# An attention kernel with a computed position bias: relus taken off GpSimd, the pair step's order of issue changed, the opening and the first weight conversions rearranged

## The chip, the cores and the metric

The kernel runs on one core of a Trainium2 chip. The metric is the device time of one execution in microseconds (us). The engines are named as the profile names them: PE (TensorE, matrix products and transposes), DVE (VectorE), ACT (ScalarE), POOL (GpSimd), and SP, whose queue issues nearly all DMAs.

## The reference, cut to what matters

```python
# attention: B, H, S, D = 2, 8, 576, 64
scores = (q @ k^T) / sqrt(D)
psi_rel = log1p(abs(pos[:, None] - pos[None, :]))
psi_i = log1p(maximum(pos[:, None], 1.0))
h = maximum((psi_rel / psi_i)[..., None] @ w1 + b1, 0.0)   # 32 hidden values for each pair of positions
scores = scores + (h @ w2)                                 # 8 heads, one bias for both batches
attn = exp(scores - max); attn = attn / (sum(attn) + 1e-09)
x = attn @ v                                               # 1152 tokens x 512
# two feed-forward layers after it
x = ((x @ w_a) * (x @ w_b)) @ w_out                        # d_ff 1536
hh = x @ w_in; solu = hh * softmax(hh)                     # d_ff 1024
out = layernorm(solu) * g_ln @ w_out2
```

The feed-forward weights come in 64-bit words and are converted on the chip. Products that must be exact in 32 bits are taken as three products of split values, a high part and the rest.

## The kernel before, in words

The bias is made tile by tile, 36 tiles T = 0 to 35 of 16 positions each. For a tile, `bias_hidden(T)` writes four arrays `h` of 128 x 576: a shifted window of a table `tabs` plus one scalar per partition, then a relu. The table `HIDDEN` says which engine makes each of the four: "v" is DVE, "p" POOL (both L365), "a" ACT (L363). `bias_sums(T)` multiplies them with w2 on PE into a PSUM tile `bps` (16 matmuls, L373). `bias_out(T)` evicts it with ACT into `st` (L383), and a DMA on the SP queue writes it into the bias array of its 128 rows (L385). Eight tiles make one such array.

The opening loop makes T = 0 to 8 and, between them, seven pieces of transposed q and k: `piece` transposes on PE into the one PSUM tile of the pool `ps_t` (tag t), `high` rounds it on ACT to the high part (`qhi`, `khi`, L308), and `lower` subtracts on DVE for the rest (`qlo` L317, `klo` L313). Then the SP queue gets the DMAs for the next q, the k of batch 1 and the v.

The main loop has 39 steps m, one for a pair of heads of one unit (128 rows of one batch; the ninth unit holds the last 64 rows of both batches). Software pipelining spreads a pair over four steps: in step m the scores, bias and exponentials of pair m, the reciprocal and shares of pair m - 1, the transposes of pair m - 2, and the values product of pair m - 3. Each engine works in the order in which the code issues. In a step with a bias tile, this order is:

- PE: scores of the first head (L401), scores of the second head, tail transposes (L439) and transposes of the next q (L275) into the second head's tile, sixteen transposes into `pt` (L450), values into `px` (L482), bias sums (L373).
- DVE: `biased` for both heads (scores plus bias with a running minimum, L415), the reciprocal of pair m - 1 (L428), half of `et` (L464), `qlo` (L317), the relus of the next tile (L365).
- ACT: exponential of the first head (L422), `ett` (L455), `qhi` (L308), exponential of the second head, half of `et` (L464), a relu of the next tile (L363), the eviction `st` (L383).
- POOL: the add before the reciprocal (L427), the two shares `e` times `rec` (L433), a relu (L365).

The pool `ps_s` has two PSUM tiles (tag s), and each step takes three in turn: the first head's scores, the second head's, and the bias sums. The second head's scores take the tile that the bias sums of the step before held, so they wait for its eviction.

```python
for T in range(N0 + 1):          # opening, N0 = 8
    bias_hidden(T)
    if T > 0:
        bias_sums(T - 1)
        bias_out(T - 1)
```

When a unit's fourth values product is done, `inputs_high` rounds `px` with ACT (`xhi`, L488) and `inputs_low` subtracts with DVE (`xlo`, L493), both at the end of the same step. `EARLY` puts three blocks of the first feed-forward product (`gated`, matmuls of L128) into the last steps; for them four pieces of w_a and w_b are converted in the late steps by `first_one`, in six stages each, placed by `FIRST` in half steps (64 is step 32): load, `held` on ACT (L94), `brought` (clamp, L98) with a first bit operation (L107), two more bit operations on DVE (L109, L110), the high part on ACT (L577), the rest on DVE (L579). After the loop the feed-forward part runs with PE as its steady user.

Of the kernel before, what the change touches and what calls it, by code (L numbers as in the profile page):

```python
# [17 lines left out]
P = 128  # L18
# [10 lines left out]
HIDDEN = (("pvav", "vvav", "pvva", "pvvv"),)  # L29

LOADS = ((0, 1), (1, 1), (2, 2), (3, 2))
FIRST = ((-7, -5, -3, 1, 2, 3), (-6, -4, -2, 3, 4, 5), (-5, 0, 2, 5, 6, 7), (2, 4, 5, 6, 8, 9))
# [18 lines left out]
def tile_kernel(ctx, tc, q, k, v, w1, b1, w2, w_a, w_b, w_out, w_in2, w_out2, g_ln, psi, rpsi, out):  # L51
# [108 lines left out]
    with ExitStack() as actx:  # L160
# [158 lines left out]
        def piece(w):  # L319

            src, at, g, c = w
            ps = ps_t.tile([P, 2, 512], F32, tag="t", name=f"tp_{'_'.join(map(str, w))}")
            nat = fetched[w]
            if src == "q":
                turn(ps, 0, nat, range(HG))
                return q_views(at, g, 0, ps, 0) + q_views(at, g, 1, ps, 2 * HF), -scale
            turn(ps, 0, nat, range(HG), (0, 1) if c < NK else (at,))
            return k_views(at, g, c, ps, 0), 1.0
# [19 lines left out]
        def bias_hidden(T, engines="vpa"):  # L348

            it, r, c = place(T)  # L350
            kinds = HIDDEN[min(it, len(HIDDEN) - 1)]
            kinds = kinds[T % len(kinds)]
            hs = bias_w.setdefault(T, [None] * 4)
            for qd in range(4):
                e = kinds[qd]
                if e not in engines:
                    continue
                t0 = it * P + r + 16 * qd
                h = hp.tile([P, S], F32, tag="h", name=f"h_{T}_{qd}")
                win = tb[:, OFF - t0 - c:OFF - t0 - c + S]  # L360
                sc = nb[:, c, t0 // 16:t0 // 16 + 1]
                if e == "a":
                    nc.scalar.activation(h, win, AF.Relu, bias=sc)  # L363
                else:
                    (nc.vector if e == "v" else nc.gpsimd).tensor_scalar(h, win, sc, 0.0, op0=ALU.add, op1=ALU.max)  # L365
                hs[qd] = h
# [147 lines left out]
        for T in range(N0 + 1):  # L514
            if T == N0 - 2:
                halves_l = table(low, half - low, psi_l, low - 12, ps_s, "s")
                nc.scalar.copy(*halves_l[0])
                nc.vector.tensor_copy(*halves_l[1])
            bias_hidden(T)
            if T > 0:  # L520
                bias_sums(T - 1)
                bias_out(T - 1)
            if done:
                lower(*done)
                done = None
            if T > 0 and order:
                done = piece(order.pop(0))
                high(*done)
# [3 lines left out]
        if done:  # L532
            lower(*done)
        bias_sums(N0)
        bias_out(N0)
        for g in range(2):
            fetch(("q", 1, g, 0))
        for w in ks[1][:3]:
            fetch(w)
        for p in range(-1, 2):  # L540
            load_v(0, p)
        for w in ks[1][3:]:
            fetch(w)
        for p in range(2, HP):
            load_v(0, p)

# [16 lines left out]
        def first_one(i):  # L563
# [6 lines left out]
            held(words, f)  # L570
            yield
            brought(f, nc.vector)
# [6 lines left out]
            nc.vector.tensor_tensor(out=lo, in0=f, in1=hi.bitcast(F32), op=ALU.subtract)  # L579
# [22 lines left out]

        bias_hidden(sums_at[0])
        NP = len(pairs)
        for m in range(NP + LAG + 1):
# [21 lines left out]
            if now:  # L627
                biased(u, 2 * p)
                powers(u, 2 * p)
                biased(u, 2 * p + 1)  # L630
            if last:
                summed_powers(*last)
            if up:
# [7 lines left out]
            if up:  # L641
                turned(*up)
            if out_:
                values(*out_)
            if T is not None:
                bias_sums(T)
            if up:
                kept(*up, 1)
                kept(*up, 0)
            lower(views, -scale)  # L650
# [3 lines left out]
            if T is not None:  # L654
                bias_out(T)
# [4 lines left out]
            if out_ and out_[1] == HP - 1:  # L660
                inputs_high(out_[0])
                inputs_low(out_[0])
            if now and p > 1 and u + 2 < NU:
                fetch(("q", u + 2, p - 2, 0))
            others(2 * m + 1)

# [340 lines left out]
```

## Time and profile before

| | |
|---|---|
| median of three runs | 570.29 us (570.04 to 570.39) |
| the profiled execution | 570.18 us, span 568.2 us |
| mean granted TensorE clock | 0.976 |
| busy, share of the span | PE 90%, DVE 74%, ACT 50%, POOL 36% |

The span runs from the first to the last instruction; 2.0 us of the execution lie around it. Busy shares are means over an opening, an attention loop and a feed-forward part with different limits, so the stretches are read one by one.

### The profile page before, as it was taken

To read this page: it belongs to the slowest core of one execution; us is meant where nothing else is said; L and a number is where in the kernel's file an instruction comes from. 1 tells how busy PE (TensorE), PEld (TensorE's weight loads), DVE (VectorE), ACT (ScalarE), POOL (GpSimd) and SP (SyncE) were. 2 spreads that over 40 slices of the span, in tenths; PEclk is the share of its full clock that TensorE was granted. 3 is DMA by queue.
4 is the path that set the end of the run, shared out by engine and by line. 5 is a ranking of instruction groups with operands and counts; after the bars stand their busy time and mean duration, and the time that the engine had idled before them with its cause. 6 is when DMAs were issued, how large, how long until landed. Compare 5 with 4: busy or idle time off the path is not lost.

```text
span 568.2 us, 13476 instructions
## 1 busy us (share of the span) xinstructions
PE 513.5 (90%) x5416; PEld 448.9 (79%) x5416; DVE 420.6 (74%) x864; ACT 281.4 (50%) x607; POOL 201.8 (36%) x235
## 2 busy tenths in 40 slices
PE   5766888888877986999999999999999999999997
PEld 2334666666665876999999999999999988888886
DVE  4847888978986596369789889889785566765661
ACT  4745787777776654345555524451352533223231
POOL 5815667666656444022222212224121630000000
PEclk9987999989999798999999999999999999999999
DMA  5469543333355410064444434345320000000001
GB/s 130 123 154 220 116 102 84 85 80 84 84 117 136 127 40 2 2 197 146 142 148 149 148 112 149 112 144 153 112 76 1 0 1 18 20 19 20 20 18 55
DMA packets 63521, 51.75 MB, mean 91 GB/s; under 512 B 41182, under 2 KB 53731, under 8 KB 63460
## 3 DMA queue, kind: packets, MB, share of 16 engines
q1 hardware_dynamic: 63184, 50.88, 32.7%
q8 instruction: 42, 0.69, 0.5%
q14 instruction: 19, 0.16, 0.1%
q10 hardware_dynamic: 276, 0.02, 0.0%
HBM read 36.73 MB, written 2.36 MB: 69 GB/s over the span
## 4 chain that ended last, share of the span: by engine, by line
PE 67%; DVE 14%; ACT 10%; issue 4%; DMA 2%; SPq 1%; POOL 1%; DVEq 0%; ACTq 0%; POOLq 0%
PE pm L128 25%; PE po L128 13%; PE py L904 9%; PE ph L844 9%; DVE e L415 4%; DVE h L365 4%; ACT st L383 3%; PE s L401 2%; PE bps L373 2%; PE px L482 2%; ACT h L363 2%; DVE qlo L317 2%; ACT et L464 2%; ACT e L422 1%; PE pl L885 1%
## 5 line engine op out<-in xcount | busy, mean ns | idle before, releaser
L98 POOL TENSOR_SCALAR f<-f 128x512 f32<-128x512 f32 x48 | 41.3, 861 | 142.7 <-ACT f L94 135.9
L433 POOL TENSOR_SCALAR e<-e,rec 128x576 f32<-128x576 f32 x72 | 55.1, 778 | 70.6 <-DVE rec L428 70.6
L128 PE MATMUL pm<-xhi,abh 128*128 128x384 f32 x240 | 80.2, 334 | 0.0
L128 PE MATMUL pm<-xhi,abl 128*128 128x384 f32 x240 | 80.2, 334 | 0.0
L128 PE MATMUL pm<-xlo,abh 128*128 128x384 f32 x240 | 80.2, 334 | 0.0
L422 ACT ACTIVATE e<-e,nm 128x576 f32<-128x576 f32 x72 | 55.9, 776 | 43.0 <-DVE nm L415 31.4
L365 POOL TENSOR_SCALAR h<-tabs 128x576 f32<-128x576 f32 x27 | 64.9, 2406 | 8.2 <-PE bps L373 5.4
L415 DVE CUSTOM_DVE_ANT_0 e<-s,bias 128x576 f32<-128x576 f32 x72 | 52.6, 751 | 20.6 <-PE s L275 14.0
L365 DVE TENSOR_SCALAR h<-tabs 128x576 f32<-128x576 f32 x90 | 62.7, 745 | 2.8 <-PE bps L373 2.8
L373 PE MATMUL bps<-h,w2bd 128*32 128x288 f32 x576 | 47.2, 446 | 3.2 <-POOL h L365 3.1
L128 PE MATMUL po<-gh,oh 128*128 128x384 f32 x144 | 48.5, 337 | 0.6 <-DVE x2s L775 0.6
L128 PE MATMUL po<-gh,ol 128*128 128x384 f32 x144 | 48.4, 336 | 0.0
L128 PE MATMUL po<-gl,oh 128*128 128x384 f32 x144 | 48.4, 336 | 0.0
L128 PEld LDWEIGHTS pm<-xhi,abh 128*128 128x128 f32 x240 | 45.1, 188 | 0.0
L128 PEld LDWEIGHTS pm<-xlo,abh 128*128 128x128 f32 x240 | 45.1, 188 | 0.0
L128 PEld LDWEIGHTS pm<-xhi,abl 128*128 128x128 f32 x240 | 45.1, 188 | 0.0
L401 PE MATMUL s<-khi,qhi 64*128 64x288 f32 x128 | 26.0, 400 | 20.8 <-ACT st L383 17.9
L401 PEld LDWEIGHTS s<-khi,qhi 64*128 64x128 f32 x128 | 12.6, 190 | 40.6 <-ACT st L383 24.6
L110 DVE SCALAR_TENSOR_TENSOR f<-words,f 128x512 int32<-128x512 int32 x48 | 42.9, 893 | 1.6
L147 ACT COPY one<-pm 128x384 f32<-128x384 f32 x36 | 17.1, 476 | 50.3 <-PE pm L128 50.3
L482 PE MATMUL px<-et,vsb 128*32 128x128 f32 (+1 forms) x1280 | 41.5, 275 | 0.0
L94 ACT ACTIVATE f<-words 128x512 f32<-128x512 f32 x48 | 32.4, 676 | 17.9 <-DMA words<-in_moe_w_out_dram 6.9
(149 smaller groups left out, 1247.6 us busy)
## 6 DMA issues: line engine op xcount, KB each, us to landing
bias<-st SPq DMA_DIRECT2D x40, 288.0 KB, 3.5
words<-in_moe_w_out_dram SPq DMA_DIRECT2D x20, 512.0 KB, 3.6
words<-in_moe_w_a_dram SPq DMA_DIRECT2D x12, 512.0 KB, 3.6
words<-in_moe_w_b_dram SPq DMA_DIRECT2D x12, 512.0 KB, 3.6
nat_q<-in_q_dram SPq DMA_DIRECT2D x32, 128.0 KB, 3.5
words<-in_moe_w_in_dram SPq DMA_DIRECT2D x8, 512.0 KB, 3.6
arena<-in_k_dram SPq DMA_DIRECT2D x16, 128.0 KB, 3.9
vsb<-in_v_dram SPq DMA_DIRECT2D x16, 128.0 KB, 3.0
```

The lines of the kernel that those rows point to most:

```text
L98: engine.tensor_scalar(f, f, WORD_MAX, WORD_MIN, op0=ALU.min, op1=ALU.max)
L110: nc.vector.scalar_tensor_tensor(out=b, in0=words[:, :, 0], scalar=29, in1=b, op0=ALU.logical_shift_right, op1=ALU.bitwise_or)
L128: nc.tensor.matmul(ps, w, x, start=(i == 0), stop=(i == n - 1))
L365: (nc.vector if e == "v" else nc.gpsimd).tensor_scalar(h, win, sc, 0.0, op0=ALU.add, op1=ALU.max)
L373: nc.tensor.matmul(bps[32 * qd:32 * qd + 32, a, 0:SH], w2bd, h[:, a * SH:(a + 1) * SH], start=True, stop=True)
L401: nc.tensor.matmul(ps[:, a, 0:SH], w[r], x[r, b, h, :], start=(i == 0), stop=(i == len(mm) - 1))
L415: nc.vector.tensor_tensor_reduce(out=halves(e), in0=ps[:, :, 0:SH], in1=halves(bias_t[it][:, h, :]), op0=ALU.add, op1=ALU.min, scale=1.0, ...
L422: nc.scalar.activation(e, e, AF.Exp, bias=nm, scale=-1.0, accum_out=sums[:, h:h + 1])
L433: nc.gpsimd.tensor_scalar(e, e, rec[:, h:h + 1], 1.0, op0=ALU.mult, op1=ALU.mult)
L482: nc.tensor.matmul(px[rows, p, cols], lhsT, rhs, start=(c == 0 and m == 0), stop=(c == NC), skip_group_check=True)
L844: nc.tensor.matmul(ph[u][:, a], x[:, kc, cols], w[:, kc, a * 512:(a + 1) * 512], start=(i == 0), stop=(i == 3 * KD - 1))
L904: nc.tensor.matmul(ps, x[:, c, :], w[:, c, cols], start=(i == 0), stop=(i == 3 * KF - 1))
```

## The change

Five edits. No relu is made on POOL any more: `HIDDEN` holds only "v" and "a", with a row of its own for the first eight tiles. In the pair step the bias sums go ahead of the values on PE, the eviction of the sums goes ahead of half of `et` and the relu on ACT, and `inputs_low` moves into the next step. The reciprocal goes between the two `biased` of DVE. The opening loop ends at T = 7 and makes only four of the seven pieces in it; the other three, tile 8 and the DMAs are issued after it. In `first_one`, the clamp and the last subtraction go to GpSimd, and the stages are placed anew.

```diff
--- before.py
+++ after.py
@@ -26,10 +26,10 @@
 
 LAG = 2
 
-HIDDEN = (("pvav", "vvav", "pvva", "pvvv"),)
+HIDDEN = (("vvva", "vava", "vvva", "vavv", "vvva", "vavv", "vvva", "vavv"), ("vvav", "vvvv", "vavv", "vvva"))
 
 LOADS = ((0, 1), (1, 1), (2, 2), (3, 2))
-FIRST = ((-7, -5, -3, 1, 2, 3), (-6, -4, -2, 3, 4, 5), (-5, 0, 2, 5, 6, 7), (2, 4, 5, 6, 8, 9))
+FIRST = ((-7, -5, -4, -1, 0, 1), (-6, -4, -2, 1, 2, 3), (-5, -2, 0, 3, 4, 5), (0, 2, 4, 6, 7, 8))
 
 
 SUMS = (6, 5, 5)
@@ -316,10 +316,10 @@
                 for l_, p_, h_ in parts_:
                     nc.vector.scalar_tensor_tensor(out=l_, in0=p_, scalar=by, in1=h_.bitcast(F32), op0=ALU.mult, op1=ALU.subtract)
 
-        def piece(w):
+        def piece(w, pool=ps_t, tag="t"):
 
             src, at, g, c = w
-            ps = ps_t.tile([P, 2, 512], F32, tag="t", name=f"tp_{'_'.join(map(str, w))}")
+            ps = pool.tile([P, 2, 512], F32, tag=tag, name=f"tp_{'_'.join(map(str, w))}")
             nat = fetched[w]
             if src == "q":
                 turn(ps, 0, nat, range(HG))
@@ -345,24 +345,21 @@
             it, r = divmod(T, P // 16)
             return it, 64 * (r // 4), r % 4
 
-        def bias_hidden(T, engines="vpa"):
+        def bias_hidden(T):
 
             it, r, c = place(T)
             kinds = HIDDEN[min(it, len(HIDDEN) - 1)]
             kinds = kinds[T % len(kinds)]
             hs = bias_w.setdefault(T, [None] * 4)
             for qd in range(4):
-                e = kinds[qd]
-                if e not in engines:
-                    continue
                 t0 = it * P + r + 16 * qd
                 h = hp.tile([P, S], F32, tag="h", name=f"h_{T}_{qd}")
                 win = tb[:, OFF - t0 - c:OFF - t0 - c + S]
                 sc = nb[:, c, t0 // 16:t0 // 16 + 1]
-                if e == "a":
+                if kinds[qd] == "a":
                     nc.scalar.activation(h, win, AF.Relu, bias=sc)
                 else:
-                    (nc.vector if e == "v" else nc.gpsimd).tensor_scalar(h, win, sc, 0.0, op0=ALU.add, op1=ALU.max)
+                    nc.vector.tensor_scalar(h, win, sc, 0.0, op0=ALU.add, op1=ALU.max)
                 hs[qd] = h
 
         def bias_sums(T):
@@ -511,38 +508,50 @@
             fetch(w)
         N0 = P // 16
         done = None
-        for T in range(N0 + 1):
-            if T == N0 - 2:
-                halves_l = table(low, half - low, psi_l, low - 12, ps_s, "s")
-                nc.scalar.copy(*halves_l[0])
-                nc.vector.tensor_copy(*halves_l[1])
+        for T in range(N0):
             bias_hidden(T)
             if T > 0:
                 bias_sums(T - 1)
                 bias_out(T - 1)
+            if T == N0 - 2:
+                halves_l = table(low, half - low, psi_l, low - 12, ps_t, "t")
+            if T == N0 - 1:
+                nc.scalar.copy(*halves_l[0])
+                nc.vector.tensor_copy(*halves_l[1])
             if done:
                 lower(*done)
                 done = None
-            if T > 0 and order:
+            if T > 0 and len(order) > 3:
                 done = piece(order.pop(0))
                 high(*done)
             if T == 1:
                 for j in range(2):
                     nc.gpsimd.memset(vtl[(1 - j) * TL:(2 - j) * TL, :, :, j, :], 0.0)
-        if done:
-            lower(*done)
-        bias_sums(N0)
-        bias_out(N0)
+        assert done is None and len(order) == 3
+        bias_sums(N0 - 1)
+        bias_out(N0 - 1)
+        for w in ks[1][:2]:
+            fetch(w)
         for g in range(2):
             fetch(("q", 1, g, 0))
-        for w in ks[1][:3]:
-            fetch(w)
         for p in range(-1, 2):
             load_v(0, p)
-        for w in ks[1][3:]:
+        for w in ks[1][2:]:
             fetch(w)
         for p in range(2, HP):
             load_v(0, p)
+        bias_hidden(N0)
+        made = piece(order[0])
+        high(*made)
+        lower(*made)
+        made = piece(order[1])
+        high(*made)
+        lower(*made)
+        bias_sums(N0)
+        made = piece(order[2])
+        high(*made)
+        lower(*made)
+        bias_out(N0)
 
         sums_at, keys_at, extra = {}, {}, {}
 
@@ -568,15 +577,15 @@
             yield
             f = pools[0].tile([P, NW], F32, tag="gl" if i < 3 else "gh", name=f"single_{i}")
             held(words, f)
+            brought(f, nc.gpsimd)
             yield
-            brought(f, nc.vector)
             yield from single(words, f)
             if not first:
                 first.append(big.tile([P, 2, 2, 2, NW], F32R, tag="big", name="first"))
             hi, lo = (first[0][:, j, c, m] for j in range(2))
             nc.scalar.copy(hi, f)
             yield
-            nc.vector.tensor_tensor(out=lo, in0=f, in1=hi.bitcast(F32), op=ALU.subtract)
+            nc.gpsimd.tensor_tensor(out=lo, in0=f, in1=hi.bitcast(F32), op=ALU.subtract)
             if m == 1:
                 w_ab[c] = tuple([first[0][:, j, c, l].rearrange("p (k f) -> p k f", k=KD) for l in range(2)] for j in range(2))
             yield
@@ -600,6 +609,7 @@
             for f, args in extra.pop(n, []):
                 f(*args)
 
+        gone = []
         bias_hidden(sums_at[0])
         NP = len(pairs)
         for m in range(NP + LAG + 1):
@@ -627,9 +637,10 @@
             if now:
                 biased(u, 2 * p)
                 powers(u, 2 * p)
-                biased(u, 2 * p + 1)
             if last:
                 summed_powers(*last)
+            if now:
+                biased(u, 2 * p + 1)
             if up:
                 kept_tails(*up, spare)
             high(views, -scale)
@@ -640,29 +651,33 @@
                     shares(last[0], 2 * last[1] + h)
             if up:
                 turned(*up)
+            if T is not None:
+                bias_sums(T)
             if out_:
                 values(*out_)
-            if T is not None:
-                bias_sums(T)
             if up:
                 kept(*up, 1)
+            lower(views, -scale)
+            if gone:
+                inputs_low(gone.pop())
+            if T is not None:
+                bias_out(T)
+            if up:
                 kept(*up, 0)
-            lower(views, -scale)
             others(2 * m)
             if after is not None:
                 bias_hidden(after)
-            if T is not None:
-                bias_out(T)
             for w in keys_at.get(m, []):
                 made = piece(w)
                 high(*made)
                 lower(*made)
             if out_ and out_[1] == HP - 1:
                 inputs_high(out_[0])
-                inputs_low(out_[0])
+                gone.append(out_[0])
             if now and p > 1 and u + 2 < NU:
                 fetch(("q", u + 2, p - 2, 0))
             others(2 * m + 1)
+        inputs_low(gone.pop())
 
 
     w2p = ctx.enter_context(tc.tile_pool(name="w2p", bufs=1, side="right"))
```

## Rows read from the trace of the kernel before

**Rows 1.** Stages: length; busy (count) of PE, PEld, DVE, ACT, POOL; clock; DMA
```profile
0.00:33.71 33.71, 22.21 (x280) 10.61 (x280) 20.15 (x41) 18.38 (x31) 22.30 (x22) 0.95 0.53 127
33.71:60.94 27.23, 18.51 (x246) 12.85 (x246) 18.45 (x45) 16.17 (x36) 10.29 (x12) 0.81 0.82 179
60.94:178.29 117.35, 98.42 (x2084) 76.96 (x2085) 102.05 (x246) 88.45 (x206) 80.21 (x88) 0.99 0.42 97
178.29:189.03 10.74, 7.70 (x134) 6.32 (x131) 5.24 (x17) 5.24 (x15) 3.84 (x8) 0.75 0.67 178
189.03:212.77 23.74, 20.67 (x462) 18.07 (x460) 19.75 (x49) 15.30 (x41) 11.42 (x20) 0.97 0.20 59
212.77:220.82 8.05, 4.22 (x122) 3.52 (x122) 5.36 (x14) 3.83 (x9) 1.66 (x3) 1.00 0.01 2
```
**Rows 2.** Groups by line, 60.94 to 178.29: count, busy, mean ns, idle before
```profile
L365 DVE TENSOR_SCALAR h<-tabs 128x576 f32<-128x576 f32 x55 | 41.0, 793 | 0.0
L365 POOL TENSOR_SCALAR h<-tabs 128x576 f32<-128x576 f32 x17 | 40.9, 2405 | 0.0
...
L401 PE MATMUL s<-khi,qhi 64*128 64x288 f32 x92 | 18.4, 396 | 18.8 <-ACT st L383 17.3 <-DVE qlo L317 1.5
```
**Rows 3.** Timeline of two steps: start, length, engine, what, idle before and releaser
```profile
105.88 0.74 DVE L415 CUSTOM_DVE_ANT_0 e<-s,bias 128x576 f32<-128x576 f32 x1
...
106.25 0.40 PE L401 MATMUL s<-khi,qhi 64*128 64x288 f32 x2 [0.71 <-ACT st L383]
...
107.14 0.76 DVE L415 CUSTOM_DVE_ANT_0 e<-s,bias 128x576 f32<-128x576 f32 x1 [0.51 <-PE s L275]
...
108.08 1.46 POOL L433 TENSOR_SCALAR e<-e,rec 128x576 f32<-128x576 f32 x2 [0.69 <-DVE rec L428]
...
108.65 1.19 PE L373 MATMUL bps<-h,w2bd 128*32 128x288 f32 x16
...
108.99 2.21 DVE L365 TENSOR_SCALAR h<-tabs 128x576 f32<-128x576 f32 x3
...
109.52 2.41 POOL L365 TENSOR_SCALAR h<-tabs 128x576 f32<-128x576 f32 x1
...
111.12 0.74 DVE L415 CUSTOM_DVE_ANT_0 e<-s,bias 128x576 f32<-128x576 f32 x1
...
112.01 0.19 POOL L427 TENSOR_SCALAR rec<-sums 128x2 f32<-128x2 f32 x1
...
113.71 1.70 DVE L365 TENSOR_SCALAR h<-tabs 128x576 f32<-128x576 f32 x2
...
116.32 0.69 DVE L493 TENSOR_TENSOR xlo<-px,xhi 128x512 fp32r<-128x512 f32 x1 [0.90 <-ACT xhi L488]
```
**Rows 4.** Timeline of the opening up to the first pair step
```profile
9.24 2.17 PE L373 MATMUL bps<-h,w2bd 128*32 128x288 f32 x16 [3.15 <-POOL h L365]
...
18.87 1.20 PE L373 MATMUL bps<-h,w2bd 128*32 128x288 f32 x16
...
22.48 0.94 DVE L365 TENSOR_SCALAR h<-tabs 128x576 f32<-128x576 f32 x2
...
29.53 0.74 ACT L383 ACTIVATE st<-bps,rp 128x576 f32<-128x576 f32 x1 [1.00 <-ACT h L363]
...
32.23 2.47 SPq L256 DMA_DIRECT2D nat_q<-in_q_dram  x4
...
36.82 0.48 PE L275 MATMUL s<-ident,nat_q 64*128 64x64 f32 x4 [4.49 <-DMA nat_q<-in_q_dram]
```
**Rows 5.** Timeline around the last pair step
```profile
217.49 0.69 DVE L493 TENSOR_TENSOR xlo<-px,xhi 128x512 fp32r<-128x512 f32 x1 [2.62 <-ACT xhi L488]
...
221.63 0.69 PE L128 MATMUL pm<-xhi,first 128*128 128x384 f32 x1 [3.57 <-DVE nm L415]
```
**Rows 6.** Groups by line, whole span: the conversions' subtraction on DVE, a like one on POOL
```profile
L924 POOL TENSOR_TENSOR wo_lo<-wo,wo_hi 128x512 fp32r<-128x512 f32 x8 | 10.4, 1297 | 9.3 <-ACT wo_hi L923 9.3
...
L579 DVE TENSOR_TENSOR first<-single,first 128x512 fp32r<-128x512 f32 x4 | 2.7, 685 | 0.1
```

## The prediction

> **What bounds the kernel now.** I read the table of stages first, cut where the first biased operation of steps 0, 4, 27, 29, 34 and 35 starts [rows 1]. What lies behind 220.82 is feed-forward work that the change does not touch, so it moves as a block. Ahead of it no engine is full. From step 4 to step 27, 23 steps take 117.35 us, 5.10 each, of which PE is busy 4.28 (98.42 / 23), DVE 4.44, ACT 3.85 and POOL 3.49. So the loop is tied by waits between engines with nearly equal loads, DVE nearest to full.
>
> The groups by line say which waits [rows 2]. PE's first matmul of a score waits 17.3 us in that stretch for the eviction `st`. DVE's relus have a mean of 793 ns, POOL's 2405. The timeline of two steps shows how this closes a loop [rows 3]: ACT evicts the sums late, the second head's scores start at 106.25 after 0.71 of waiting, and DVE stands 0.51 at 107.14 for these scores. Then DVE makes its relus beside POOL's shares and relu: three in 2.21, or two in 1.70. Once per unit it also waits 0.90 for `xhi` before `xlo` (116.32). In the opening, the timeline shows PE waiting 3.15 for POOL's first relu, and 4.49 for the next q, whose DMAs stand behind the bias DMAs [rows 4].
>
> **The change part by part: the middle (steps 4 to 27).** A step of DVE without a wait runs from 111.12 to 113.71 up to its relus: 2.59, the reciprocal included [rows 3]. For the tiles made here `HIDDEN` gives DVE 13 relus in four tiles (before 10) and ACT 3, as before. What does a relu cost with POOL quiet? A pair that ran before POOL's next relu took 0.94, so 0.47 each, write-back included [rows 4]. The other end is the mean of 0.793 [rows 2]. I take 0.47: POOL's shares (1.46 for two) start right behind the reciprocal, which moves ahead of the second biased operation, so they start one such operation (0.74) sooner. Counted from the step's start, they ran from 2.20 to 3.66 (108.08 less 105.88) in a step that held a wait of 0.51; without that wait and 0.74 sooner they run from about 0.95 to 2.41, and the relus start at 2.59 [rows 3]. Four steps then cost 4 x 2.59 + 13 x 0.47 + 0.69 for `xlo` = 17.16, or 4.29 each.
>
> Two waits must go for that to hold. The second scores waited for `st`, and the eviction now stands ahead of half of `et` and of ACT's relu, with its sums one values product sooner on PE; so PE should have no reason to pause there. Queued behind `st` on ACT is now half of `et`, which the next step's transposes need free and its values need written; both come a good part of a step later. Behind the sums on PE are the values, which wait for nothing new; the sums themselves need the first biased operation done earlier, and it ended at 106.62, over 2 us before they started at 108.65. `xlo` waits for nothing once it stands a step later; it meets the tile with four DVE relus (2.59 + 0.69 + 1.88 = 5.16), 0.87 over the mean, which the three steps of 2.59 + 1.41 = 4.00 give back. PE's busy 4.28 per step is as high, and ACT's 3.85 fits: no engine is asked for more than 4.29. Gain: (5.10 - 4.29) x 23 = 18.6. Bounds: 22 if PE's bursts, once joined, lose some fill time (an estimate, 4.15 per step); 9 if a relu costs 0.60, between the two ends (4.71 per step).
>
> One row bears on the relus' price from the other side. POOL's relu ran from 109.52 to 111.93, and DVE's three beside it ended at 111.20: slowed, not stopped [rows 3]. The Trainium skill (SBUF — State Buffer, "Who interferes with whom") says that the port pair of the two engines is an exclusive lock, held for the whole instruction, and the other blocks fully; this trace disagrees for these relus. By the rows POOL's small add (0.19 at 112.01), which would fall among the new relus, costs next to nothing. By the rule it would stop DVE each time, 23 x 0.19 = 4.4 us, and the sum below would read 544.0.
>
> **The opening.** The first sums waited for POOL's relu, and five tiles' sums started 9.63 apart from first to fifth, 2.41 per tile (9.24, 18.87) [rows 4]. With DVE and ACT alone I start 2 us sooner, at 7.2, and take 2.1 per tile: three relus (1.41) and one subtraction of the `L579` kind (0.69). Tile 7's sums then start at 21.9 and its eviction at 23.1, not 29.53. The next q's DMAs started at 32.23; now they stand behind tile 7's bias DMA and four of k (0.62 each, q's own pace) but not behind tile 8: 23.1 + 0.74 + 5 x 0.62 = 26.9. They reached PE 4.59 later before (36.82), so at 31.5: 5.3 sooner. The three pieces left over run one behind the other through PE, ACT and DVE. At 2.41 each, as a tile with a piece took, they end near 30.3, so the wait for q covers them; without that cover, each 1 us more is 1 us later. Tile 8's DMA passes behind 26 loads (some 16 us at 0.62). Its eviction buffer is wanted again four tiles later, in step 3, and its rows in step 8, so this is free. Steps 1 to 3 gain from the relus (0.32 each for eight of them, 2.6), but their key pieces form a chain of their own; I take 1.2. Sum 6.5; bounds 2 (only the start) and 9.
>
> **The late steps.** From 178.29 to 189.03 PE waits for the last unit's q and its clock is granted at 0.75 on the mean, so part of it at 1.2 instead of 2.4 GHz [rows 1]. These DMAs hang on tile 35's eviction; I leave this stretch as it is. From 189.03 to 220.82, 31.8 us, DVE is busy 25.1 and PE 24.9. `xlo` waits there 2.62 for `xhi` [rows 5], which waits behind ACT's conversions; a step later the wait is gone. The clamp and the subtraction leave DVE, the latter 0.685 each, so for four pieces at most 4 x 2 x 0.685 = 5.5. POOL gets them at about 1.3 each for the subtraction [rows 6], off PE's path, but in front of the next add. PE's 24.9 is the floor, so at most 6.9 is to be had. I take 5.5, with 1 as the other end (POOL's queue holding the reciprocals). The first early block, which waited 3.57 for DVE's biased operation [rows 5], then starts that much sooner, and all behind it.
>
> **Sum.** 6.5 + 18.6 + 5.5 = 30.6. The profiled execution took 570.18 (its span 568.2 and 2.0 around it), 0.1 under the median: 570.2 - 30.6 = 539.6.
>
> **The rivals.** (1) *The reciprocal holds DVE.* It now stands between the biased operations, so a late add on POOL stops the second one, and all of DVE behind it. At 108.08 the shares had waited 0.69, so POOL was free at 107.39, 0.77 after the first biased operation ended (106.62) [rows 3]. If the add stays this late, it costs 0.77 x 23 = 17.7: 557.3. The kernel gets slower than before only where each of 36 steps loses 30.6 / 36 = 0.85 to it. Against it: POOL's relu ended at 111.93 and the add came at 112.01 directly behind it, and this relu is gone. (2) *Relus stay at 0.793*, because shares and relus still meet: (10.36 + 10.31 + 0.69) / 4 = 5.34 per step, 5.5 lost in the middle, 563.7 in all. Against it stands the pair of 0.94. (3) *Only the middle gains*: the opening gives 2 because the serial pieces or the DMAs take over, the late steps 1: 548.6. For it: many small waits stand one behind the other there. (4) *The pause before 189.03 shrinks too*, to 7 us of its 10.74, as the eviction comes sooner in its step: 535.9.
>
> **How the numbers follow.** The forecast 0.58, (4) 0.10, (3) 0.13, (2) 0.07, (1) at its measured lateness 0.04; (1) beyond its turning point, slower, 0.05; what is left, 0.03, for no change, within 0.2%, about what a measurement of this kernel can tell. Faster: 0.92. The range goes from 530 ((4) with the middle and the opening at their best, 3.4 and 2.5 more) to 556; above it lie (1), (2), no change and slower, 0.19.
>
> **What would show it.** The distance from step 4's first biased operation to step 27's should be near 99; DVE relus near 0.5; PE's wait for `st` and DVE's for `xhi` nearly gone; step 0's second biased operation near 32. A DVE wait on POOL's `rec` in most steps would prove (1), relus near 0.8 (2). I am wrong in the main point if the middle stays above 110.

## The result and the profile after

The changed kernel takes 543.24 us (median of four runs, 542.91 to 545.0) against 570.19 for the kernel before on the same chip. The ratio is 0.9533, with a 95% interval of 0.9512 to 0.9554. The forecast was 539.6 in a range of 530 to 556.

The profiled execution took 545.0, the longest of the four. Its span is 543.2, so 25.0 us under the span before (the medians differ by 26.95). The table of stages shows where they come from. It is cut at the same events as [rows 1]: the first biased operation of steps 0, 4, 27, 29, 34 and 35, in the same columns.

```profile
0.00:30.84 30.84, 21.56 (x280) 11.32 (x280) 19.08 (x47) 19.03 (x33) 2.86 (x14) 0.94 0.76 168
30.84:56.77 25.93, 20.15 (x246) 14.54 (x246) 17.90 (x48) 16.38 (x36) 5.50 (x10) 0.68 0.67 150
56.77:153.42 96.65, 92.50 (x2062) 75.19 (x2064) 91.67 (x261) 86.13 (x206) 38.91 (x70) 1.00 0.51 119
153.42:163.94 10.52, 8.00 (x152) 6.62 (x150) 6.00 (x18) 5.97 (x17) 4.30 (x8) 0.84 0.63 160
163.94:188.35 24.41, 20.62 (x422) 17.54 (x418) 18.55 (x47) 15.87 (x43) 13.94 (x23) 0.93 0.21 67
188.35:193.15 4.80, 3.20 (x70) 2.70 (x68) 2.77 (x8) 2.50 (x7) 3.52 (x5) 1.00 0.00 0
```

The middle fell from 117.35 to 96.65 us. PE is busy 92.50 of it, 96%, where it was 98.42 of 117.35. The stretch from step 29 to step 35 went only from 31.79 to 29.21, though DVE sheds 3.8 us there (25.11 before, 18.55 + 2.77 now), and from step 35 to the first early block it is 3.52 where it was 0.81. Cut at the events of the prediction, the account reads:

| stretch | before | after | gained | forecast |
|---|---|---|---|---|
| start to step 0's second biased operation | 37.34 | 31.88 | 5.46 | 5.3 |
| from there to step 4 | 23.60 | 24.89 | -1.29 | 1.2 |
| step 4 to step 27 | 117.35 | 96.65 | 20.70 | 18.6 |
| step 27 to the first early block | 43.34 | 43.25 | 0.1 | 5.5 |
| all behind it | 346.57 | 346.53 | 0.0 | 0 |

Groups by line of the middle of the changed kernel, which answer to [rows 2]:

```profile
L362 DVE TENSOR_SCALAR h<-tabs 128x576 f32<-128x576 f32 x71 | 32.3, 514 | 0.0
L398 PE MATMUL s<-khi,qhi 64*128 64x288 f32 x92 | 17.2, 370 | 0.3
L490 DVE TENSOR_TENSOR xlo<-px,xhi 128x512 fp32r<-128x512 f32 x5 | 3.4, 682 | 0.0
```

PE's 17.3 us of waiting for the eviction are gone from its matmuls (0.3 of idle time is left), `xlo` waits for nothing, and a relu costs 514 ns, not 793. The timeline of a step, which answers to [rows 3], shows how the parts now lie:

```profile
98.68 0.76 DVE L412 CUSTOM_DVE_ANT_0 e<-s,bias 128x576 f32<-128x576 f32 x1
...
99.69 1.46 POOL L430 TENSOR_SCALAR e<-e,rec 128x576 f32<-128x576 f32 x2 [1.74 <-DVE rec L425]
...
101.28 1.37 DVE L362 TENSOR_SCALAR h<-tabs 128x576 f32<-128x576 f32 x3
...
101.49 0.73 ACT L380 ACTIVATE st<-bps,rp 128x576 f32<-128x576 f32 x1
...
101.68 0.19 POOL L424 TENSOR_SCALAR rec<-sums 128x2 f32<-128x2 f32 x1 [0.53 <-ACT e L419]
...
101.86 0.40 PE L398 MATMUL s<-khi,qhi 64*128 64x288 f32 x2
...
102.57 0.76 DVE L412 CUSTOM_DVE_ANT_0 e<-s,bias 128x576 f32<-128x576 f32 x1
```

The shares end at 101.15, before the relus begin at 101.28. `st` is done at 102.22, while PE is still on the first head's scores. The second head's scores follow without a pause. DVE goes from the first biased operation of one step to that of the next in 3.89 us with three relus. Five kernels of these experiments have the same code up to step 27 (this one, the one with the conversions alone back on DVE, and the three with the reciprocal last from there on, one of them run twice); their six profiles have a middle of 96.50 to 96.87.

In the late steps the timeline shows a new wait. Two of its places:

```profile
169.94 0.61 POOL L98 TENSOR_SCALAR single<-single 128x512 f32<-128x512 f32 x1 [1.76 <-ACT single L94]
...
170.63 0.19 POOL L424 TENSOR_SCALAR rec<-sums 128x2 f32<-128x2 f32 x1
170.85 0.17 DVE L425 RECIPROCAL rec<-rec 128x2 f32<-128x2 f32 x1 [1.61 <-POOL rec L424]
...
189.56 1.28 POOL L588 TENSOR_TENSOR first<-single,first 128x512 fp32r<-128x512 f32 x1
...
190.91 0.19 POOL L424 TENSOR_SCALAR rec<-sums 128x2 f32<-128x2 f32 x1
191.14 0.17 DVE L425 RECIPROCAL rec<-rec 128x2 f32<-128x2 f32 x1 [2.03 <-POOL rec L424]
```

POOL's queue holds a conversion ahead of the add. The reciprocal waits for the add, and the second biased operation, at 170.97 and 191.26, waits behind the reciprocal. The list of waits from 153 to 197 sums this up (us in total, times, longest):

```profile
DVE rec L425 <- POOL rec L424: 10.1, 7, 2.0
```

### The profile page after: what moved, and what is told of

Read it like the earlier page. It is cut to its first block, busy times and chain, and to the rows that moved or that the text cites. A ratio compares the mean times of both kernels' runs of the same rounds, so it can differ in the third digit from the quotient of the medians.

```text
span 543.2 us, 13461 instructions
## 1 busy us (share of the span) xinstructions
PE 510.3 (94%) x5416; PEld 450.5 (83%) x5416; DVE 404.3 (74%) x880; ACT 280.9 (52%) x610; POOL 143.0 (26%) x216
## 4 chain that ended last, share of the span: by engine, by line
PE 69%; DVE 9%; ACT 9%; DMA 4%; issue 4%; SPq 2%; POOL 1%; DVEq 0%; ACTq 0%
PE pm L128 26%; PE po L128 11%; PE py L919 9%; PE ph L859 9%; PE bps L370 4%; ACT e L419 3%; DVE h L362 3%; PE px L479 3%; PE s L398 2%; DMA nat_q<-in_q_dram 2%; PE pl L900 1%; PE pt L447 1%; DMA words<-in_moe_w_out_dram 1%; ACT qhi L308 1%; DVE e L412 1%
## 5 line engine op out<-in xcount | busy, mean ns | idle before, releaser
L430 POOL TENSOR_SCALAR e<-e,rec 128x576 f32<-128x576 f32 x72 | 52.9, 746 | 64.5 <-DVE rec L425 58.5
L412 DVE CUSTOM_DVE_ANT_0 e<-s,bias 128x576 f32<-128x576 f32 x72 | 53.9, 749 | 5.6 <-PE s L398 3.1
L362 DVE TENSOR_SCALAR h<-tabs 128x576 f32<-128x576 f32 x114 | 51.8, 515 | 0.7 <-PE bps L370 0.6
L110 DVE SCALAR_TENSOR_TENSOR f<-words,f 128x512 int32<-128x512 int32 x48 | 42.8, 891 | 1.6
L94 ACT ACTIVATE f<-words 128x512 f32<-128x512 f32 x48 | 32.4, 675 | 18.6 <-DMA words<-in_moe_w_a_dram 7.4
L479 PEld LDWEIGHTS px<-et,vsb 128*32 128x32 f32 x1280 | 35.7, 116 | 5.9 <-issue 0.8
L874 ACT ACTIVATE ev<-ph,small 128x512 f32<-128x512 f32 x18 | 12.2, 684 | 49.7 <-DVE small L871 49.6
L109 DVE SCALAR_TENSOR_TENSOR f<-words,f 128x512 int32<-128x512 int32 x48 | 34.1, 710 | 1.3
```

The lines of the kernel that those rows point to most:

```text
L109: nc.vector.scalar_tensor_tensor(out=b, in0=words[:, :, 1], scalar=-0x40000000, in1=b, op0=ALU.bitwise_and, op1=ALU.bitwise_or)
L110: nc.vector.scalar_tensor_tensor(out=b, in0=words[:, :, 0], scalar=29, in1=b, op0=ALU.logical_shift_right, op1=ALU.bitwise_or)
L362: nc.vector.tensor_scalar(h, win, sc, 0.0, op0=ALU.add, op1=ALU.max)
L412: nc.vector.tensor_tensor_reduce(out=halves(e), in0=ps[:, :, 0:SH], in1=halves(bias_t[it][:, h, :]), op0=ALU.add, op1=ALU.min, scale=1.0, ...
L430: nc.gpsimd.tensor_scalar(e, e, rec[:, h:h + 1], 1.0, op0=ALU.mult, op1=ALU.mult)
L479: nc.tensor.matmul(px[rows, p, cols], lhsT, rhs, start=(c == 0 and m == 0), stop=(c == NC), skip_group_check=True)
```

## The experiments

Ratios are to the kernel before on the same chip, with 95% intervals. "Middle" is step 4 to step 27 and "late" is step 27 to the first early block, both between first biased operations as above (changed kernel: 96.65 and 43.25).

**Relus against order.** Two runs complete a square: the changed kernel with the relus given out as before, and the kernel before with only the relus taken off POOL.

```diff
-HIDDEN = (("vvva", "vava", "vvva", "vavv", "vvva", "vavv", "vvva", "vavv"), ("vvav", "vvvv", "vavv", "vvva"))
+HIDDEN = (("pvav", "vvav", "pvva", "pvvv"),)
...
-                    nc.vector.tensor_scalar(h, win, sc, 0.0, op0=ALU.add, op1=ALU.max)
+                    (nc.vector if kinds[qd] == "v" else nc.gpsimd).tensor_scalar(h, win, sc, 0.0, op0=ALU.add, op1=ALU.max)
```

> The changed kernel with the relus given out as before (27 of 144 on POOL), all else as changed. Main theory: contended DVE relus and the late eviction are two separate losses of the middle, and here only the first is back. Ten DVE relus in four tiles at about 0.75 give (4 x 2.59 + 10 x 0.75 + 0.69) / 4 = 4.64 per step instead of the measured 4.20, so 10 us over 23 steps, and about 5 in the opening: 558 (553 to 563). Rival A, the order of issue alone made the gain: under 546. Rival B, the relus alone made it: about 568 to 570.

The second run is the kernel before with the new `HIDDEN` alone (the upper line of that diff, the other way).

> The kernel before with only the new table of relu engines (none on POOL). Main theory: DVE's relus fall from 0.79 to about 0.52 each, but the second scores still wait for the eviction and xlo for xhi, so a step costs about 4.9 instead of 5.10, and the opening gains some 4: 558 to 565. Rival A (order alone): 568 or more. Rival B (relus alone): 545 to 550.

Measured: 550.80 us for the first, ratio 0.9659 (0.9628 to 0.9690); 567.44 for the second, 0.9942 (0.9916 to 0.9968). Neither fits an expectation: the first lies under the 553 of the main theory and over the 546 of the order alone, the second between 565 and 568.

| | relus on POOL too | relus off POOL |
|---|---|---|
| middle, old order | 117.35 (before) | 116.30 |
| middle, new order | 99.85 | 96.65 (after) |
| step 0's second biased, old order | 37.34 (before) | 33.66 |
| step 0's second biased, new order | 37.72 | 31.88 (after) |

In the middle the relus bring 1.05 or 3.20 us, the order 17.50 or 19.65. In the opening it is the other way round: the relus bring 3.68 or 5.84, and the new order by itself nothing. The group rows of the middle say why, first of the changed kernel with POOL's relus, then of the kernel before without them:

```profile
L362 POOL TENSOR_SCALAR h<-tabs 128x576 f32<-128x576 f32 x17 | 38.9, 2286 | 0.0
L362 DVE TENSOR_SCALAR h<-tabs 128x576 f32<-128x576 f32 x55 | 30.5, 603 | 0.0
```

```profile
L365 DVE TENSOR_SCALAR h<-tabs 128x576 f32<-128x576 f32 x71 | 40.8, 629 | 0.0
L401 PE MATMUL s<-khi,qhi 64*128 64x288 f32 x92 | 18.4, 396 | 19.2 <-ACT st L383 17.8 <-DVE qlo L317 1.5
```

With POOL still at relus but the new order, DVE's relus cost 603 ns, and there are only 10 of them in four tiles: 10 x 0.603 = 6.03 us, against 13 x 0.514 = 6.68 when DVE has them all. So the move off POOL does not lighten DVE at all. What it brings in the new order shows in the waits of the middle with POOL's relus:

```profile
DVE rec L425 <- POOL rec L424: 4.4, 15, 0.4
```

The add stands behind POOL's relu, and the reciprocal, now ahead of the second biased operation, holds DVE for it 4.4 us in all, where the changed kernel has no such wait in the middle; 3.20 are lost. And with the old order PE waits its 17.8 us for `st` whether or not POOL makes relus.

**The sums and their eviction behind the values, as before.** All else is as in the changed kernel.

```diff
-            if T is not None:
-                bias_sums(T)
             if out_:
                 values(*out_)
+            if T is not None:
+                bias_sums(T)
...
-            if T is not None:
-                bias_out(T)
             if up:
                 kept(*up, 0)
             others(2 * m)
             if after is not None:
                 bias_hidden(after)
+            if T is not None:
+                bias_out(T)
```

> The changed kernel with the bias sums behind the values and their eviction behind half of et and the relu, as before; the deferred xlo, the reciprocal's place and the relus stay as changed. Theory after the first runs: the order of issue made nearly all of the middle's gain, and the eviction's place the larger part of it, by PE's and DVE's waits: 7 to 10 us lost in the middle, 550 to 553. Rival: the deferred xlo and the early reciprocal carry it, as the relus and shares no longer meet: under 547.

Measured: 558.61, ratio 0.9790 (0.9762 to 0.9818); the middle 111.71, 15.06 more, well over the 7 to 10 expected. Group rows of its middle:

```profile
L362 DVE TENSOR_SCALAR h<-tabs 128x576 f32<-128x576 f32 x71 | 32.3, 512 | 0.0
L398 PE MATMUL s<-khi,qhi 64*128 64x288 f32 x90 | 18.0, 397 | 15.5 <-ACT st L380 15.5
```

The relus stay at 512 ns, and the wait for `st` is back, 15.5 us in 22 times. This edit holds most of the gain, and cheap relus do not replace it. How much of it is the sums' place on PE and how much the eviction's on ACT, no run separates.

**`xlo` in the step of `xhi`, as before.**

```diff
-            if gone:
-                inputs_low(gone.pop())
...
                 inputs_high(out_[0])
-                gone.append(out_[0])
+                inputs_low(out_[0])
```

> The changed kernel with xlo in the same step as xhi, as before. Theory: DVE waits 0.9 or more for xhi once per unit, six times in the middle, and xlo then stands in a step whose relus are three, so 5 to 6 us in the middle and 1 to 2 late: 549 to 551. Rival: the wait fits in DVE's slack, as the step of four relus is relieved by 0.7: under 545.

Measured: 548.76, ratio 0.9612 (0.9583 to 0.9640); the middle 102.61, 5.96 more for six units' subtractions. Two rows of the waits in its middle:

```profile
PE bps L370 <- DVE nm L412: 9.2, 10, 1.7
DVE xlo L490 <- ACT xhi L485: 8.0, 6, 1.9
```

DVE stands at `xlo` six times, 8.0 us in all, and the late biased operations then hold the sums on PE (9.2 us, where the changed kernel has 2.6). The late stretch, where 1 to 2 us more had been expected, is 40.77, 2.48 shorter than in the changed kernel: steps 27 and 28 take 7.82 against 10.52. Why is not shown.

**The reciprocal behind both biased operations, as before.**

```diff
-            if last:
-                summed_powers(*last)
             if now:
                 biased(u, 2 * p + 1)
+            if last:
+                summed_powers(*last)
```

> The changed kernel with the reciprocal behind both biased operations again. Theory: from step 27 on the reciprocal waits for an add that stands behind clamps, subtractions and memsets on POOL, and with it the second biased operation waits; here that operation goes ahead, so the late steps (39.7 us from step 27 to 35) shrink by 3 to 5 us. In the middle the shares start one operation later and end near the first relu, up to 0.2 per step where DVE sets the pace: 0 to 4 us lost. In all 539 to 545. Rival: the place of the reciprocal costs nothing late, since everything on DVE is only shifted: 543 with late steps as long as they are now, or 547 if the middle loses its full 0.2 per step.

Measured: 542.25, ratio 0.9504 (0.9476 to 0.9532), so about the time of the changed kernel; but the middle is 100.29, 3.64 longer, and the late stretch 38.43, 4.82 shorter. One group row of its middle:

```profile
L362 DVE TENSOR_SCALAR h<-tabs 128x576 f32<-128x576 f32 x71 | 38.3, 594 | 0.0
```

In the middle the early reciprocal is worth 80 ns per relu in the mean (71 x 0.080 = 5.7 us of DVE, of which 3.6 show), because it moves POOL's shares from under the relus: here 17 of the 71 run across the end of the shares and take 0.86 to 0.90, and the others take 0.50 to 0.54. In the late steps the same place costs 4.8.

**The reciprocal last from step 27 on only.** This takes each place where it pays.

```diff
-            if last:
+            if last and not (m > 26):
                 summed_powers(*last)
             if now:
                 biased(u, 2 * p + 1)
+            if last and (m > 26):
+                summed_powers(*last)
```

> The changed kernel with the reciprocal behind both biased operations from step 27 on only. Theory: the early place is worth 3.6 us in the middle (100.29 with the late place, 96.65 with the early one) and costs 4.8 in the late steps (38.43 against 43.25 from step 27 to the first early block), where POOL's queue is full; taking each where it is good gives 543.2 - 4.8 = 538.4 (537 to 540). Rival: the late steps gained in the earlier run only because a slower middle left time for loads and conversions: 542 to 543.5.

> The changed kernel with the reciprocal last from step 27 on, the same kernel as ran at 539.3, beside the two versions with further repairs on one chip: 539 to 540.

Measured: 539.30, ratio 0.9452 (0.9422 to 0.9482), and in a second run of the same kernel 539.37, 0.9453 (0.9421 to 0.9484). Both are as expected, and both intervals lie below that of the changed kernel (0.9512 to 0.9554), so this beats both kernels. The middle keeps its 96.65, and the late stretch takes 38.78. Its waits from 153 to 197:

```profile
DVE rec L425 <- POOL rec L424: 2.5, 5, 0.9
```

**Further repairs of the late steps.** Beside that version ran two more: one with the memsets of the last unit's q behind POOL's shares, and one that also has clamp and last subtraction back on DVE. The conversions alone had been put back on DVE in an earlier run.

```diff
-            brought(f, nc.gpsimd)
             yield
+            brought(f, nc.vector)
             yield from single(words, f)
...
-            nc.gpsimd.tensor_tensor(out=lo, in0=f, in1=hi.bitcast(F32), op=ALU.subtract)
+            nc.vector.tensor_tensor(out=lo, in0=f, in1=hi.bitcast(F32), op=ALU.subtract)
```

> The changed kernel with the clamp and the last subtraction of the early conversions back on DVE, stages placed as in the change. Theory (POOL's queue holds the reciprocals in the late steps): DVE's waits for the reciprocal's add from step 30 on, 1.6, 1.2, 0.8, 2.0 and 1.8 us in the profile, go under 0.3 each, and DVE gets some 5 us more work, part of it in time it now waits: 539 to 542.5. Rival (DVE's work is the limit there, as I reckoned): 545 to 548.

```diff
-                if (u, p) in ((NU - 3, HP - 1), (NU - 2, 1)):
-                    clear_q(NU - 1, NU - 2 - u == 0)
...
                     shares(last[0], 2 * last[1] + h)
+            if now and (u, p) in ((NU - 3, HP - 1), (NU - 2, 1)):
+                clear_q(NU - 1, NU - 2 - u == 0)
```

> The changed kernel with the reciprocal last from step 27 on and the memsets behind the shares; conversions stay on POOL. Theory A: POOL's memsets held the add 0.83 and 1.75 us in steps 28 and 30; with the reciprocal last only the shares wait for it, so 0 to 1.5 us are to be had, 537.8 to 539.3. Rival B: those waits are covered by the pause for q, no difference from the reciprocal alone, 539.3.

> The changed kernel with the reciprocal behind both biased operations from step 27 on, the memsets of the last unit's q behind POOL's shares, and clamp and last subtraction back on DVE. Theory A (the late steps are held by POOL: its conversions and memsets stand ahead of the add of the reciprocal): the three repairs take away the same wait, so they add up only in part; step 27 to the first early block 37.5 to 38.5 us (38.78 with the reciprocal alone), 538 to 539. Rival B (DVE is the engine that ends last there, as the prediction had it): 5.5 us of conversions come back to DVE, 41 us or more for the stretch and 541 or more in all.

Measured: conversions on DVE alone 541.53, 0.9490 (0.9458 to 0.9523), late 41.49. Reciprocal and memsets 540.60, 0.9471 (0.9443 to 0.9499), late 39.33. All three 542.27, 0.9501 (0.9469 to 0.9533), late 39.94. None is better than the reciprocal alone, and the gains expected of the last two did not come: once DVE no longer stands long at it (2.5 us instead of 10.1), what POOL has ahead of the add costs little, and nothing is gained by giving DVE the conversions back.

**One key piece per step.** The pieces of batch 1, two of which share a step twice, are spread over steps 1 to 5.

```diff
-        for m, w in zip((1, 1, 2, 2, 3), ks[1]):
+        for m, w in zip((1, 2, 3, 4, 5), ks[1]):
```

> The changed kernel with the five key pieces of batch 1 made one per step in steps 1 to 5, not two, two and one in steps 1 to 3. Theory: in steps 1 and 2 the second piece's chain through PE, ACT and DVE (about 2.1 us) stands bare at the end of the step, so two such go, and steps 4 and 5 get one piece each, which costs there about 1: 540 to 541.5. Rival: PE's granted clock of 0.68 in these steps sets their length, whatever the pieces: 543 or more.

Measured: 544.76, ratio 0.9545 (0.9507 to 0.9583): no gain, where one was expected. Steps 1 to 4 of this kernel in the table of stages:

```profile
35.57:41.21 5.64, 4.65 (x52) 3.03 (x52) 3.99 (x11) 4.34 (x9) 1.66 (x3) 0.78 0.95 215
41.21:46.97 5.76, 3.35 (x58) 2.41 (x58) 4.48 (x13) 4.33 (x10) 1.66 (x3) 1.00 0.69 170
46.97:53.01 6.04, 4.40 (x86) 3.33 (x88) 4.73 (x15) 3.55 (x9) 1.66 (x3) 1.00 0.73 160
53.01:58.83 5.82, 4.74 (x110) 3.90 (x106) 4.48 (x12) 4.33 (x10) 1.66 (x3) 1.00 0.61 131
```

Five steps of 5.6 to 6.5 us (35.57 to 65.36) replace three of 6.7 to 7.7 and two of 3.9 (29.79 in all, changed kernel 29.59), and from step 6 to step 27 another 0.95 is lost (89.78, changed kernel 88.83). PE's clock is granted in full in three of the four rows (0.72, 0.73 and 0.70 in steps 1 to 3 of the changed kernel), and still no engine is busy over 5 us of a step. So neither the doubling nor PE's clock alone is what these steps cost.

**The opening's order as before.** Nine tiles and seven pieces are made in the loop again, the low table goes through the other pool, and the q's DMAs stand behind tile 8; the relus stay off POOL.

```diff
-        for T in range(N0):
+        for T in range(N0 + 1):
...
-            if T > 0 and len(order) > 3:
+            if T > 0 and order:
                 done = piece(order.pop(0))
...
-        for w in ks[1][:2]:
-            fetch(w)
         for g in range(2):
             fetch(("q", 1, g, 0))
...
-        bias_hidden(N0)
-        made = piece(order[0])
...
```

> The changed kernel with the opening's order as before: nine tiles and seven pieces in the loop, the low table at tile 6 through the other pool, the q DMAs behind tile 8. The relus stay on DVE and ACT. Theory A (the order of the opening is worth about a third of its gain, the relus the rest): as in the kernel before with its relus off POOL, step 0's second biased operation near 33.7 (31.9 in the changed kernel), step 4 near 58.4 (56.8), 544.8 in all. Rival B (the three pieces behind the loop cost as much as the earlier q gives): step 4 near 56.8, 543.2.

Measured: 547.12, ratio 0.9585 (0.9557 to 0.9613), more than either theory had; step 0's second biased operation at 35.00, step 4 at 60.13. One row of its opening's timeline, and one of its table of stages:

```profile
34.48 0.48 PE L275 MATMUL s<-ident,nat_q 64*128 64x64 f32 x4 [4.19 <-DMA nat_q<-in_q_dram]
```

```profile
24.00:26.00 2.00, 2.00 (x26) 0.76 (x19) 1.23 (x3) 1.05 (x3) 0.00 (x0) 0.55 0.05 13
```

PE waits 4.19 for q again. By this run the new order of the opening is worth 3.1 us at the place where q is awaited (35.00 less 31.88), and the relus the other 2.3. But the kernel before without POOL's relus has the same opening code and was there at 33.66. PE's granted clock differs between the two: 0.55 from 24 to 26 here, 1.00 there. So of the 5.46 the order's part is 1.8 to 3.1, the relus' 3.7 to 2.3.

## Why the prediction was right, and where it was not

**The opening: right, with two errors that cancel.** The timeline of the changed kernel's opening answers to [rows 4]:

```profile
7.12 2.85 PE L370 MATMUL bps<-h,w2bd 128*32 128x288 f32 x16 [0.95 <-DVE h L362]
...
22.19 0.74 ACT L380 ACTIVATE st<-bps,rp 128x576 f32<-128x576 f32 x1
...
26.04 3.06 SPq L256 DMA_DIRECT2D nat_q<-in_q_dram  x4
...
28.51 0.69 DVE L313 TENSOR_TENSOR klo<-tp_k,khi 128x512 fp32r<-128x512 f32 x1 [1.42 <-ACT khi L308]
...
31.37 0.47 PE L275 MATMUL s<-ident,nat_q 64*128 64x64 f32 x4 [1.12 <-DMA nat_q<-in_q_dram]
```

The first sums start at 7.12 (forecast 7.2), tile 7's eviction at 22.19 (23.1), q's DMAs at 26.04 (26.9), and q is used at 31.37 (31.5). That last agreement is in part luck: the DMAs started 0.9 sooner than forecast and took 5.33 to reach PE, where 4.59 was taken. In nine other profiles of this opening code step 0's second biased operation comes at 31.76 to 32.52, so the gain is 4.8 to 5.6. The last piece ends at 29.20 (30.3), under the cover of q's wait, of which 1.12 is left.

**Steps 1 to 3: the step that failed is "gain from the relus"**, 1.2 by forecast and -1.29 measured. DVE does not end last there. The timeline of step 2 of the changed kernel shows what does:

```profile
45.23 1.37 DVE L362 TENSOR_SCALAR h<-tabs 128x576 f32<-128x576 f32 x3
...
46.06 0.59 ACT L461 COPY et<-pt 128x512 f32<-128x512 f32 x1
...
46.70 0.46 PE L275 MATMUL tp_k<-ident,arena 64*128 64x64 f32 x4 [1.49 <-ACT et L461]
...
47.63 0.42 DVE L313 TENSOR_TENSOR klo<-tp_k,khi 128x256 fp32r<-128x256 f32 x1 [1.03 <-ACT khi L308]
...
49.47 0.69 DVE L313 TENSOR_TENSOR klo<-tp_k,khi 128x512 fp32r<-128x512 f32 x1 [1.42 <-ACT khi L308]
```

The pieces run through PE, ACT and DVE one behind the other and end the step. DVE has finished its relus at 46.60 and stands 1.03 for the first piece's `khi` and 1.42 for the second's. A cheaper relu only lengthens these waits. The first piece now waits 1.49 for half of `et`, which stands behind the eviction on ACT. Steps 1 to 3 take 20.52 us before, 21.57 with the relus alone changed, 20.24 with all but the relus changed, and 21.77 after. That the relus off POOL cost the 1.1 to 1.5 us is not shown by this: the five other profiles of the same code up to step 27 have 21.12 to 21.98. Step 3 of the changed kernel, and of the one with all three late repairs:

```profile
50.08:56.77 6.69, 6.45 (x108) 4.84 (x104) 4.98 (x14) 3.87 (x9) 1.66 (x3) 0.70 0.44 90
```

```profile
50.18:56.00 5.82, 5.05 (x108) 4.19 (x104) 4.92 (x14) 3.77 (x9) 1.67 (x3) 0.91 0.50 104
```

With POOL's relus step 3 took 5.82 too, at a clock of 0.92. So the 0.87 by which the changed kernel's step 3 is longer goes with PE's clock, not with the relus. Of the rest, 0.66 in step 1, the cause stays open.

**The middle: the sum was right, its split between causes was not.** Forecast 4.29 us per step, measured 4.20. DVE's base of 2.59 is 2.60 in the step shown (98.68 to 101.28), and three relus take 1.37 there, 0.46 each, where 0.47 was taken. The two waits went as the prediction said, and so did the shares, which the earlier reciprocal moved from under the relus (594 ns against 514 by its place alone). What the runs correct is the relus' weight: at 0.60 each the prediction left 9 us of the gain, and with 594 ns 17.1 came (117.35 to 100.29). Undone one at a time, the sums and eviction cost 15.1, `xlo` 6.0, the reciprocal's place 3.6 and the relus' 3.2. That is 27.9 for a gain of 20.7, so the edits need one another. For the relus a run shows it: alone they bring 1.05, as PE still waits for `st`. The other edits were not run alone.

**The add among the relus.** By the rule of the Trainium skill (SBUF — State Buffer, "Who interferes with whom") POOL's add would have stopped DVE at each relu group, and the sum would have been 544.0. The measured time is close to that, but not by this way: the add at 101.68 runs within the three relus that start at 101.28, and they take 1.37, 0.46 each, no more than the pair of [rows 4] with POOL still. All 71 DVE relus of the middle take 0.51 to 0.52, the 34 that meet the add included. The rule's stop does not show in this trace; what the span lacks of the forecast gain (30.6 less 25.0) are 5.4 in the late steps and 2.5 in steps 1 to 3, less 2.1 that the middle and 0.2 that the opening gave beyond the forecast.

**The late steps: the step that failed is the 5.5 for work shed by DVE**, measured 0.1. The other end given, 1, was the one that came. The prediction named the mechanism there, POOL's queue holding the reciprocals, and took the wrong end: the wait is rival (1), absent in the middle and present here. In the middle the add is done early, at 101.87, before the next step begins at 102.57. In the late steps a clamp, a subtraction of 1.27 to 1.51 (forecast 1.3) or a memset stands ahead of it, seven times for 10.1 us. DVE did shed work, and stood still instead. With the reciprocal last from step 27 on, 4.5 us come (43.25 to 38.78), but even then hardly for the work shed: with clamp and subtraction on DVE again the stretch is 39.94, only 0.6 to 1.2 more than without (39.33 with the memsets moved, 38.78 alone). Which of the other edits brought the remaining 3.4 against the kernel before, no run separates.

**The rivals.** (2) fell: no run of the changed order had a mean of the middle's relus above 603 ns. (3) fell for the opening, which kept 4.2 net of steps 1 to 3, and held for the late steps. (4) fell: step 27 to step 29 took 10.52 us, before 10.74. Rival (1) holds in seven late steps of the changed kernel, and in the middle only where POOL still makes relus.

## What to carry to other kernels

Read the chain that closes from one step to the next, not the busiest engine: here sums and an eviction issued sooner in their step were worth more (15.1 us of the middle when undone) than the relus taken off GpSimd (3.2 there). An instruction moved forward in an engine's order takes its own wait with it; check its releaser in every stage, for a place that pays in the steady loop (3.6 us) can cost as much in the tail (4.8), where that releaser's queue holds other work. When an edit makes one engine's work cheaper, look first whether that engine is the one that ends the step: in steps 1 to 3 it was not, and no gain came of it. And look at single instructions before pricing one by the mean of its group.

## What had not been expected of the hardware

The same relu (add, then maximum, 128x576 in 32 bits) takes 2.29 to 2.41 us on POOL in the mean, and 2.21 where DVE did nothing beside it (kernel before, at 30.83), while POOL's scaling of an array of that size by two factors takes 0.75 (1.46 for two). Beside POOL's work the mean of a relu on DVE rises: 514 ns with the shares moved away, 594 to 629 with the shares beside it, 793 with shares and POOL's relu. But these means mix two kinds. The three relus that [rows 3] of the kernel before merges, one by one:

```profile
108.99 0.87 DVE L365 TENSOR_SCALAR h<-tabs 128x576 f32<-128x576 f32 x1
...
109.78 0.99 DVE L365 TENSOR_SCALAR h<-tabs 128x576 f32<-128x576 f32 x1
...
110.69 0.51 DVE L365 TENSOR_SCALAR h<-tabs 128x576 f32<-128x576 f32 x1
```

The first runs across the end of POOL's shares (109.54), the second starts after POOL's relu has begun (109.52), and the third, still beside that relu (to 111.93), takes no longer than one beside an idle POOL. In that middle 22 of the 55 relus run across the end of a share and take 0.79 to 0.94, 17 are the first to start behind the start of a POOL relu and take 0.99, and the other 16 take 0.50 to 0.51. With POOL's relus in the new order it is 16 first ones of 55 that take 0.79 to 0.91, and the others 0.51 to 0.52. So only relus that meet the end of a share or the start of a POOL relu are stretched; the rest are not slowed.

From step 0 to step 4 PE's clock was granted at 0.68 in the mean after, 0.81 before. Finer cuts of the same table of stages of the changed kernel show where it fell:

```profile
24.00:27.00 3.00, 1.59 (x24) 0.83 (x24) 1.64 (x6) 0.74 (x2) 0.00 (x0) 0.97 1.09 232
27.00:29.00 2.00, 1.52 (x14) 1.17 (x14) 0.58 (x2) 1.12 (x2) 0.00 (x0) 0.50 1.28 215
...
35.00:37.00 2.00, 2.00 (x18) 1.42 (x22) 1.61 (x5) 1.36 (x3) 0.99 (x2) 0.50 0.57 129
37.00:39.00 2.00, 1.15 (x20) 0.47 (x12) 1.56 (x5) 1.98 (x5) 0.67 (x2) 0.98 1.01 224
```

PE had stood idle 2.08 us until 25.27, by the profile for the bias DMAs. From 27 to 37 us it then ran at 1.2 GHz, the lower of its two levels, while it had work. So the last of the three pieces taken out of the opening loop (its transposes take 0.69 at 27.15, those of the piece at 25.27 took 0.46), step 0 and the start of step 1 ran slow. The wait for q covered the piece; in steps 1 to 3, with 0.72, 0.73 and 0.70, PE's part of the chain had no cover.
